# Attention denominators as compact rows spread by DMA broadcasts, the output gate folded into W_o ahead of the merge, and the third modulation set moved into the W_o phase

## The chip, the cores and the metric

The kernel runs on one core of one Trainium2 chip. The metric is device time in microseconds (us), lower is better. Times are quoted as the median of several executions with the lowest and highest beside it. Each experiment was timed beside the kernel before on the same chip in the same rounds. A program on one core can also fall into slower executions; a run is labelled slow when it is more than 1.5% above the fastest run of the same kernel, and the ratios use only the runs that are not.

## The reference

One transformer block: linear attention with 32 heads, then a gated feed-forward network (FFN). Six rows computed from a condition vector `c` scale, shift and gate both halves (the *modulation*).

```python
mod = (silu(c) @ w_mod).reshape(1, 6, 1, 1024)     # sa, ca, ga, sb, cb, gb
h = layernorm(x) * (1 + ca) + sa                   # x: 2048 rows of 1024
q, k, v = split_heads(h @ wqkv)                    # 32 heads of 32 columns
pq, pk = phi(q), phi(k)                            # phi(t) = t+1 or exp(t), positive
kv  = einsum('bhsd,bhse->bhde', pk, v)             # one 32x32 matrix per head
z   = einsum('bhsd->bhd', pk)
num = einsum('bhqd,bhde->bhqe', pq, kv)
den = einsum('bhqd,bhd->bhq', pq, z)[..., None] + 1e-6   # one number per head and row
x = x + ga * ((num / den) @ wo)
h = layernorm(x) * (1 + cb) + sb
x = x + gb * ((gelu(h @ w_gate) * (h @ w_up)) @ w_down)  # F = 3584
```

## The kernel before

**A plan, then in-order engines.** The kernel first *records* every operation and then sorts the list with its own model of the chip (one DMA pipe, fixed latencies). It then issues each engine's operations in that fixed order. On the chip each engine takes its own list strictly in order: an operation that isn't ready holds up everything behind it on the same engine. A change to any operation makes the planner sort anew, so it can move operations in phases that the change doesn't touch. In the experiments, "order frozen" means that the sorted list of another kernel was written into the source as a list of operation numbers, so that only the named edit differs.

**Phases.** (1) LayerNorm, then K, V and Q for four blocks of 512 rows. (2) The merge: each head's KV matrix is multiplied into W_o once (giving `Wp`), interleaved with the last Q blocks and two modulation sets. (3) The W_o phase: 16 tiles of 128 rows, residual add, second LayerNorm; the normalised rows go to DRAM (`xhs`) and come back transposed in two DMA transposes of 1 MB. (4) For each half of the rows (0 and 1), a gate/up phase and a down phase. Both use a Strassen-like scheme, so the kernel needs sums of quarters of the weights. Those of `W_down` (`ts`) are built in DRAM by 28 copy and accumulate DMAs of 256 KB, called the *moves* here.

The denominators before: one block-diagonal matrix `Dbd` per group of four heads, so that a 128x512 matmul yields the denominator already repeated over the 32 rows of its head; then 1/den as exp(-ln(den)) on ACT, over all 128x1024 numbers.

```python
def den_pair(b, g, banks):
    psd = banks.pair()
    for i in range(2):
        te.matmul(psd[:, i, :], lhsT=Dbd[:, g + i, :], rhs=pqT[b][:, g + i, :], start=True, stop=True)
    ac.activation(out=psd, in_=psd, func=AF.Ln, bias=eps6, scale=1.0)
    rden = rden_ring()
    ac.activation(out=rden, in_=psd, func=AF.Exp, scale=-1.0)
    o = pqT[b][:, g:g + 2, :]
    tt_op(o, o, rden, ALU.mult)                     # DVE; 16 such pairs in all

def wp_step(g):                                     # merge: (KV x W_o) x gate row
    psw = psW.pair()
    for h in range(2):
        te.matmul(psw[:, h, :], lhsT=KVbdT[:, g, :], rhs=Wo_sb[:, g, h * NW:(h + 1) * NW], start=True, stop=True)
    ve.scalar_tensor_tensor(out=Wp[:, g, :], in0=psw.rearrange("p h n -> p (h n)"), scalar=1.0 / GA_SCALE,
                            in1=garow, op0=ALU.mult, op1=ALU.mult)

def wo_tile(tt, banks):
    xt = x2_ring()                                  # ring of 4 row buffers
    sy.dma_start(out=xt, in_=x_in[tt * P:(tt + 1) * P, :])
    psw = banks.pair()
    # ... 16 matmuls of pqT[b] with Wp ...
    tt_op(xt, psw.rearrange("p h n -> p (h n)"), xt, ALU.add)      # residual add, DVE
    gp.dma_start(out=x2_scr[b][tl * P:(tl + 1) * P, :], in_=xt)
    # ... ln2_xhat writes the normalised rows to xhs, and every fourth tile:
    sy.dma_start_transpose(out=hr2[:, :, h * TG:(h + 1) * TG], in_=xh_scr[g][h][:])

def plain(name, A, out, start):                     # down phase: load of a W_down quarter or sum
    wt = quarters(...)
    (sy if last or name[0] != "t" else gp).dma_start(out=wt, in_=wd_full[name])
```

`te`, `ve`, `ac`, `gp` and `sy` record for TensorE, VectorE (DVE), ScalarE (ACT), GpSimd (POOL) and SyncE (SP, which issues most DMAs). In the first down phase, loads of the sums `t...` are issued by GpSimd, all other loads by SP.

## Time and profile before

| | before |
|---|---|
| median (lowest to highest), first three runs | 758.01 us (757.61 to 759.67) |
| profiled execution: span, granted TensorE clock | 754.9 us, 1.00 |
| TensorE busy | 734.4 us, 97% of the span |
| W_o phase / gate/up 0 / down 0 | 60.8 / 170.7 / 80.7 us |

The profile page's first part gives, for each engine, busy us, share of the span and number of instructions (PEld is the weight load, which overlaps PE):

```profile
PE 734.4 (97%) x4144; PEld 391.3 (52%) x4164; DVE 623.4 (83%) x1304; ACT 411.6 (55%) x697; POOL 95.8 (13%) x175
```

The view of waits, for TensorE in the kernel before. Columns: what waited, for what, us in total, how often, longest.

```profile
PE psum L648 <- DVE mem L635: 5.5, 1, 5.5
PE psum L685 <- DMA mem<-in_c_dram: 2.2, 1, 2.2
PE psum L964 <- ACT mem L967: 1.9, 2, 1.0
PE psum L952 <- DVE mem L536: 0.7, 1, 0.7
```

The first two lines are the unavoidable start; L964 is the denominators' matmul waiting for ACT (the Exp of L967). TensorE has hardly anything else to wait for. The view by windows, one row per phase (merge and end of Q, W_o, gate/up 0, down 0, gate/up 1). The header names the columns; a number in brackets counts instructions, PEclk is the granted clock and the DMA share is the mean busy share of the 16 DMA engines:

```profile
core 0: us, PE busy (x) PEld busy (x) DVE busy (x) ACT busy (x) POOL busy (x), PEclk, DMA share, GB/s
152.50:192.90 40.40, 37.19 (x241) 17.20 (x244) 35.02 (x59) 31.29 (x36) 15.08 (x16) 1.00 0.89 214
192.90:253.70 60.80, 59.99 (x277) 27.18 (x279) 50.28 (x83) 38.37 (x55) 11.98 (x22) 1.00 0.83 244
253.70:424.40 170.70, 169.26 (x862) 84.06 (x861) 149.26 (x341) 116.99 (x220) 21.70 (x39) 1.00 0.62 204
424.40:505.10 80.70, 80.59 (x519) 50.76 (x520) 64.57 (x117) 19.63 (x30) 6.00 (x9) 1.00 0.86 257
505.10:669.80 164.70, 164.59 (x947) 92.46 (x946) 145.23 (x335) 105.97 (x221) 1.43 (x2) 1.00 0.35 107
```

In the W_o phase TensorE is busy 59.99 of 60.80 us. The timeline of this phase shows how the rows get back (columns: start us, duration us, engine, line, operation, out<-in; SPq is SP issuing a DMA):

```profile
219.25 5.32 SPq L1116 DMA_TRANSPOSE mem<-xhs  x1
225.24 0.42 SPq L1248 DMA_DIRECT2D mem<-in_B_w_gate_dram  x1
229.05 0.80 ACT L1158 ACTIVATE mem<-mem 128x512 f16<-128x512 f16 x1
```

### The profile page before, as it was taken

What the parts mean: (1) busy time and instruction counts of PE and PEld (TensorE: products, weight loads), DVE (VectorE), ACT (ScalarE), POOL (GpSimd) and SP (SyncE); (2) the same over time, 40 slices, a digit from 0 to 9 for tenths busy, and PEclk for the clock granted to TensorE, in tenths of its full rate; (3) what the DMA queues carried; (4) which work ended last, traced back from release to release, by engine and by line L of the source; (5) the groups of instructions that cost most, each with busy time, mean ns of one, the idle gap of its engine ahead of it and who ended that gap; (6) DMA issues with size and microseconds to landing.
All of it is one profiled execution on the core that took longest, in us unless ns stands there. A gap on an engine that the chain in (4) does not pass through costs nothing.

```text
span 754.9 us, 11379 instructions
## 1 busy us (share of the span) xinstructions
PE 734.4 (97%) x4144; PEld 391.3 (52%) x4164; DVE 623.4 (83%) x1304; ACT 411.6 (55%) x697; POOL 95.8 (13%) x175
## 2 busy tenths in 40 slices
PE   5999999998999999999999999999999999999997
PEld 2454544453444444444545486645555555548664
DVE  7898986579897788988998689678888899998763
ACT  3675675668866578766755243016666667621000
POOL 2331332007121003101100001010000000000000
PEclk9999999999999999999999999999999999999999
DMA  9848166789389647687652999752322313399822
GB/s 314 305 120 252 43 151 155 277 309 167 86 231 315 232 154 246 220 272 281 207 185 60 292 276 313 254 181 84 112 78 90 112 56 112 103 274 294 280 95 80
DMA packets 140760, 144.78 MB, mean 192 GB/s; under 512 B 33441, under 2 KB 120865, under 8 KB 139937
## 3 DMA queue, kind: packets, MB, share of 16 engines
q1 hardware_dynamic: 124016, 106.31, 46.8%
q0 software_dynamic: 14336, 35.66, 14.9%
q10 hardware_dynamic: 2352, 2.10, 0.8%
q8 instruction: 32, 0.52, 0.3%
q14 instruction: 24, 0.19, 0.1%
HBM read 111.81 MB, written 32.24 MB: 191 GB/s over the span
## 4 chain that ended last, share of the span: by engine, by line
PE 80%; DVE 8%; ACT 6%; DMA 4%; issue 1%; SPq 1%; DVEq 0%; ACTq 0%
PE psum L1286 28%; PE psum L1489 13%; PE psum L1533 9%; PE psum L1297 7%; DVE mem L536 7%; PE psum L838 6%; PE psum L1178 6%; PE psum L908 4%; PE psum L937 4%; DMA mem<-in_A_wqkv_dram 2%; DMA mem<-in_B_w_up_dram 1%; DMA mem<-in_w_mod_dram 1%; PE psum L952 1%; ACT psum L965 1%; ACT mem L967 1%
## 5 line engine op out<-in xcount | busy, mean ns | idle before, releaser
L536 DVE TENSOR_TENSOR mem<-mem 128x512 f16<-128x512 f16 (+11 forms) x633 | 292.5, 506 | 12.1 <-ACT mem L967 2.5
L1286 PE MATMUL psum<-mem 128*128 128x512 f16 x1248 | 299.3, 379 | 1.3 <-ACT psum L1340 0.5
L536 DVE TENSOR_TENSOR mem<-psum,mem 128x512 f16<-128x512 f32 (+4 forms) x260 | 192.3, 748 | 67.5 <-ACT mem L783 22.6
L783 ACT ACTIVATE mem<-psum 128x256 f32<-128x256 f32 (+2 forms) x228 | 123.2, 555 | 121.1 <-PE psum L1533 46.4
L1286 PEld LDWEIGHTS <-mem 128*128 128x128 f16 (+1 forms) x1248 | 122.0, 98 | 113.4 <-issue 4.0
L1489 PE MATMUL psum<-mem 128*128 128x512 f16 (+2 forms) x458 | 99.0, 372 | 0.7 <-DVE mem L536 0.5
L1297 PE MATMUL psum<-mem 128*128 128x256 f16 x560 | 89.5, 272 | 0.3
L1297 PEld LDWEIGHTS <-mem 128*128 128x128 f16 (+1 forms) x560 | 54.7, 98 | 45.7 <-issue 3.9
L1489 PEld LDWEIGHTS <-mem 128*128 128x128 f16 x462 | 45.1, 98 | 49.9 <-issue 0.7
L1533 PE MATMUL psum<-mem 128*128 128x256 f16 (+1 forms) x588 | 66.2, 273 | 0.0
L1340 ACT ACTIVATE psum<-psum 128x512 f32<-128x512 f32 x56 | 33.0, 589 | 59.0 <-PE psum L1286 31.5
L1533 PEld LDWEIGHTS <-mem 128*128 128x128 f16 x588 | 57.5, 98 | 9.2
L838 PE MATMUL psum<-mem 128*128 128x512 f16 (+1 forms) x272 | 61.6, 379 | 0.4
L1178 PE MATMUL psum<-mem 128*128 128x512 f16 x256 | 57.4, 379 | 0.8 <-DVE mem L536 0.7
L908 PE MATMUL psum<-mem 128*128 128x512 f16 x224 | 51.1, 379 | 0.1
L536 DVE TENSOR_TENSOR psum<-psum,mem 128x256 f32<-128x256 f32 x80 | 34.2, 427 | 12.3 <-ACT mem L783 12.2
L1357 ACT ACTIVATE mem<-psum 128x512 f16<-128x512 f32 x56 | 33.2, 598 | 18.8 <-PE psum L1286 18.3
L838 PEld LDWEIGHTS <-mem 128*128 128x128 f16 x280 | 27.1, 98 | 31.2
L1178 PEld LDWEIGHTS <-mem 128*128 128x128 bf16 x256 | 25.0, 98 | 31.0 <-issue 0.9
L1367 ACT ACTIVATE mem<-mem 128x512 f16<-128x512 f16 x56 | 34.9, 633 | 2.0 <-DVE mem L536 1.8
L908 PEld LDWEIGHTS <-mem 128*128 128x128 f16 (+1 forms) x224 | 21.5, 98 | 26.8 <-issue 2.1
L614 DVE BATCH_NORM_STATS2 mem<-mem 128x6 f32<-128x512 bf16 x48 | 31.0, 678 | 1.6 <-DMA mem<-in_A_x_dram 1.6
(126 smaller groups left out, 558.5 us busy)
## 6 DMA issues: line engine op xcount, KB each, us to landing
mem<-in_B_w_gate_dram SPq DMA_DIRECT2D x14, 1024.0 KB, 6.1
mem<-in_B_w_up_dram SPq DMA_DIRECT2D x14, 1024.0 KB, 5.8
mem<-in_w_mod_dram SPq DMA_DIRECT2D x24, 512.0 KB, 7.0
mem<-us SPq DMA_DIRECT2D x24, 448.0 KB, 8.0
mem<-in_A_x_dram SPq DMA_DIRECT2D x32, 256.0 KB, 4.0
ts<-in_B_w_down_dram POOLq DMA_DIRECT2D x28, 256.0 KB, 6.7
us<-mem POOLq DMA_DIRECT2D x7, 768.0 KB, 7.2
mem<-in_B_w_down_dram SPq DMA_DIRECT2D x12, 448.0 KB, 6.8
```

The costliest lines, as they stand in the source:

```text
L536: ve.tensor_tensor(out=out, in0=a, in1=b, op=op)
L783: ac.activation(out=t, in_=ps, func=AF.Copy)
L838: te.matmul(ps, lhsT=A[:, k, i * P:(i + 1) * P], rhs=B[:, k, :], start=(start and k == 0), stop=(k == KH - 1), skip_group_check=True)
L908: te.matmul(o, lhsT=W[:, k, (j0 + i) * P:(j0 + i + 1) * P], rhs=h_form(a, k), start=(start and k == 0), stop=(k == KH - 1), skip_group_che ...
L1178: te.matmul(psw[:, half, :], lhsT=pqT[b][:, g, tl * P:(tl + 1) * P], rhs=Wp[:, g, half * NW:(half + 1) * NW], start=(g == 0), stop=(g == K ...
L1286: te.matmul(ps, lhsT=a[:, k, e, :], rhs=b[:, k, :], start=(start and k == 0), stop=(k == KH - 1), skip_group_check=True)
L1297: te.matmul(ps, lhsT=self.x[a][:, k, :], rhs=self.y[y][:, k, :], start=(start and k == 0), stop=(k == KH // 2 - 1), skip_group_check=True)
L1340: ac.activation(out=z, in_=x, func=AF.Copy)
L1357: ac.activation(out=o, in_=ps, func=AF.Gelu_apprx_tanh)
L1367: ac.activation(out=o, in_=o, func=AF.Gelu_apprx_tanh)
L1489: te.matmul(psm[:, q, c], lhsT=A[:, i, q * P:(q + 1) * P], rhs=wt[:, i, c], start=(start and i == 0), stop=(i == NPR - 1), skip_group_chec ...
L1533: te.matmul(ps[:, q, :], lhsT=a[:, k, q * P:(q + 1) * P], rhs=y[:, k, :], start=(start and q == 0 and k == 0), stop=(k == NPR // 2 - 1), s ...
```

## The change

Its intent: take denominator work off TensorE (most of the sum's output rows are copies), most of the Ln/Exp off ACT, and the gate's multiply of PSUM off DVE. In detail:

- **Denominators.** 32-column matmuls put the denominators of two blocks compactly into one PSUM bank; one Ln and one Exp of 128x512 serve two blocks; the result goes to DRAM in 4 DMAs of 16 KB and comes back repeated over 32 rows, per block in 4 DMAs of 256 KB.
- **Gate.** W_o is multiplied by the gate row (16 bits, on DVE) before the merge, so the merge's PSUM is evacuated by a plain ACT copy.
- **Third modulation set.** Its load and matmuls go from the merge into the W_o phase.
- **Also in it:** the FFN's up products become an ACT copy and a 16-bit DVE multiply instead of a DVE multiply from PSUM (56 times); the 28 moves, 16 in the K/V/Q phase and 12 in the merge before, are now 14 in the K/V/Q phase and 14 in gate/up 0; the ring of row buffers grows from 4 to 8 and its loads may be issued earlier; the planner learns that the four broadcasts write one tile together. Small parts: the order of the moves, two more PSUM banks for the merge (4 to 7, not 4 and 5), the second modulation set one merge stage later, one more `c1` buffer.

```diff
-    def den_pair(b, g, banks):  (shown above, 16 calls)
+    def den_sums(pr, ps):
+        for gi in range(KH):
+            for b in range(2):
+                for half in range(2):
+                    o, g = DH * (2 * b + half), KH * half + gi
+                    te.matmul(ps[o:o + DH, :], lhsT=zc[:, g, :], rhs=pqT[2 * pr + b][:, g, :],
+                              start=(gi == 0), stop=(gi == KH - 1))
+        ac.activation(out=ps, in_=ps, func=AF.Ln, bias=eps6, scale=1.0)
+        ac.activation(out=rdc, in_=ps, func=AF.Exp, scale=-1.0)
+        # ... 4 writes of rdc to den_scr[pr]
+    def den_mul(b):
+        rden = rden_ring()
+        plan.together(True)
+        for j in range(P // DH):
+            src = den_scr[b // 2][b % 2, j].rearrange("h x -> (h x)")
+            sy.dma_start(out=rden[DH * j:DH * j + DH].rearrange("p g t -> p (g t)"),
+                         in_=src[None, :].to_broadcast((DH, KD * TG)))
+        plan.together(False)
+        for g in range(0, KD, 2):
+            o = pqT[b][:, g:g + 2, :]
+            tt_op(o, o, rden[:, g:g + 2, :], ALU.mult)
 ...
     def wp_step(g):
-            te.matmul(psw[:, h, :], lhsT=KVbdT[:, g, :], rhs=Wo_sb[:, g, h * NW:(h + 1) * NW], ...)
-        ve.scalar_tensor_tensor(out=Wp[:, g, :], in0=psw..., scalar=1.0 / GA_SCALE, in1=garow, ...)
+            te.matmul(psw[:, h, :], lhsT=KVbdT[:, g, :], rhs=Wog[:, g, h * NW:(h + 1) * NW], ...)
+        ac.activation(out=Wp[:, g, :], in_=psw..., func=AF.Copy, scale=1.0 / GA_SCALE)
 ...
     merge_phase, by stage i:
-            i == 3: load of modulation set 2;  i == 11: its matmuls;  i == 12: its columns
-            i in (6, 8, 10, 12, 13): den_pair
+            i == 5: den_sums(0, psN());  i in (8, 11): den_mul;  i == 8: load of modulation set 2
     wo_phase, by tile tt:
-            den_pair at every tile until done
+            tt == 2: matmuls of set 2;  tt == 3: den_sums(1, psX());  tt in (4, 7): den_mul
 ...
-        put(3, 1, F(wd_moves, hr1[3][:, 0, 0:1], 16))      # K/V/Q phase; 12 more in the merge
+            wd_moves(hr1[b][:, 0, 0:1], NPR)               # 14 in the K/V/Q phase
+                wd_moves(w["s1"][:, 0, 0, 0:1], 2)         # 2 per even unit of gate/up 0
 ...
-                    tt_op(o, ps, o, ALU.mult)
+                    tt_op(o, fcopy(c1_ring, ps), o, ALU.mult)
```

## The prediction

> **What bounds the kernel now.** TensorE. The page's first part shows it busy for 734 of 755 us at a granted clock of 1.00; the chain that ended last is 80% TensorE. Of its 20 us idle, about 8.8 lie in the first 25 us and 3.6 in the tail; in the table of 25 us stretches only 175 to 200 stands out between (2.9 us idle; ACT 21.4 and DVE 21.8 of 25 us busy), then 225 to 250 and 275 to 325 (0.5 to 0.7 each). The waits view names the denominators' Exp on ACT (1.9 us of TensorE waits). So time can come only from TensorE work removed or from these small gaps; the large ACT and DVE savings are mostly off the critical path.
>
> **Costs, from the trace.**
> - Denominators. Before: 32 matmuls of 128x512, spaced 0.216 us in an unbroken run: 6.9 us. After: 32 matmuls with 32 output columns; those of the modulation sets run 16 in 0.98 us, so 2.0 us. This fits the Trainium skill, "TensorEngine Tiling (Array Packing)", where narrow tiles run in parallel and a mode switch drains the array; I allow 0.2 us for each of two more switches. About -4.6 us, all critical.
> - ACT: 16 x (Ln 1.09 + Exp 1.02) = 34 us removed; added 2 x (0.6 + 0.6) and, in the merge, 8 copies of 1.02.
> - DVE in the merge: 8 x 1.22 (gate times PSUM) becomes 8 x 0.68 (gate times W_o, 16-bit); the diagonals (8 x 0.24) narrow. About -5 us. The 16 denominator multiplies stay.
> - The third modulation set's matmuls (2 us) only move.
> - DMA: four broadcasts of 1 MB, about 6 us each at the trace's 1 MB landing times, after a write of 2 to 4 us, issued several 2 us stages or 3.9 us W_o tiles before use: at most a short new wait. Of the 28 W_down moves (256 KB), 14 go to the first gate/up phase (DMA share 0.6 to 0.85, loads early): neutral.
> - FFN up products: 56 PSUM multiplies (about 0.7 us of DVE) become an ACT copy (0.6) and a 16-bit multiply (about 0.35): DVE -17 us, ACT +33, but TensorE loses only 1 to 2 us in the first gate/up phase and nearly nothing in the second.
>
> **Sum.** -4.6 from denominators, -2.5 of the 4 us or so lost in the merge, -0.6 in the W_o phase, -0.8 at the start of the FFN: about -8.5 us. Predicted 749.5 us, range 744.5 to 755. Chances: faster by over 2% 0.04, within 2% 0.94, slower 0.02.
>
> **What would show each step.** TensorE's matmul count unchanged, its gap-free time 5 us lower; denominator matmuls about 60 ns apart; ACT partly idle, not 85% busy, in the merge; no TensorE wait for the denominators' Exp; W_o phase starting some 4 us and ending 7 to 8 us earlier; second group's gate/up and down of unchanged length; DVE about 25 us less busy, ACT about level.
>
> **What would make it wrong.** (1) A new wait on the chain gate row, W_o x gate, merge, which starts just after the second half of the modulation set: the merge then gains nothing (about 752). (2) The broadcasts land late, behind the 4 MB of the third modulation set or in order behind other issues of the SP queue, so that the first W_o tile or the modulation matmuls wait several us (755 or more). (3) The new ACT copies hold up the FFN's banks or GELUs. (4) The list order, computed anew, shifts other phases by a us or two.

## The result and the profile after

| | before | after |
|---|---|---|
| median (lowest to highest), 4 runs | 757.81 us (757.08 to 759.67) | 783.78 us (781.66 to 790.27) |
| ratio of fast runs | | 1.035 (1.029 to 1.042) |
| span and clock of the profiled run | 754.9, 1.000 | 779.9, 0.985 |

Ratios are the mean time of one kernel's fast runs over that of the other's of the same rounds, so they are not quite the ratio of the medians quoted. The kernel is 3.5% slower where it was predicted 1.1% faster, and its runs scatter more: 1.1% from lowest to highest against 0.3%.

The first part of the page and the TensorE waits, after:

```profile
PE 737.8 (95%) x4164; PEld 390.8 (50%) x4164; DVE 603.2 (77%) x1304; ACT 417.2 (54%) x733; POOL 101.0 (13%) x179
...
PE psum L1214 <- DVE mem L550: 12.5, 3, 11.1
PE psum L1577 <- ACT mem L799: 5.7, 1, 5.7
PE psum L662 <- DVE mem L649: 5.6, 1, 5.6
PE psum L924 <- DVE mem L550: 2.6, 1, 2.6
PE psum L1329 <- DVE mem L550: 2.6, 1, 2.6
```

The work changed as intended: DVE is 20 us less busy and ACT about level. But TensorE has four new waits: one of 11.1 us in a W_o tile (L1214), one of 5.7 us in down 0 (L1577), and two of 2.6 us (L924 is the merge's Q, L1329 gate/up 0). The same windows by phase, after; the last one is a short stretch around the long wait:

```profile
core 0: us, PE busy (x) PEld busy (x) DVE busy (x) ACT busy (x) POOL busy (x), PEclk, DMA share, GB/s
156.80:190.80 34.00, 31.37 (x192) 13.87 (x192) 24.83 (x49) 25.77 (x32) 0.31 (x1) 0.98 0.62 198
190.80:266.10 75.30, 62.84 (x311) 27.11 (x310) 48.97 (x81) 19.12 (x37) 12.69 (x23) 0.89 0.93 248
266.10:442.00 175.90, 169.34 (x862) 84.10 (x861) 146.36 (x351) 131.40 (x249) 41.33 (x59) 1.00 0.71 215
442.00:529.90 87.90, 82.25 (x521) 51.48 (x520) 67.41 (x125) 19.49 (x30) 6.11 (x9) 0.98 0.87 232
529.90:694.60 164.70, 164.32 (x946) 92.42 (x945) 134.02 (x327) 120.75 (x249) 1.45 (x2) 1.00 0.35 106
244.20:257.90 13.70, 5.05 (x12) 1.72 (x12) 3.72 (x5) 5.75 (x8) 1.08 (x2) 0.50 1.00 243
```

By the phase table below (these windows are rounded) the 25.0 us of span divide as follows: up to the start of the W_o phase -2.1, W_o +14.6, gate/up 0 +5.2, down 0 +7.1, the rest +0.2. The DMA share in the W_o phase rose from 0.83 to 0.93 and PEclk fell to 0.89. In the last row, 13.7 us around the wait, the clock is 0.50.

That is the clock gate. The Trainium skill, "TensorE: Matmul & The Clock Gate", section "What's actually happening", says that an idle window of 3413 ns brings TensorE to half its clock and that a busy window brings it back. This trace agrees on the length of a window. After the start of the kernel, the half-clock stretches last 3.4 us (189.6 to 193.0, and 476.3 to 479.7) and 13.65 us (244.2 to 257.9, four windows); each belongs to one of the waits in the table, and the kernel before has none until its end. It does not show that the window before must be idle throughout. Cut into windows of 3.413 us in step with the start of the half-clock stretch, TensorE was still busy for 1.15 of 3.41 us in the window before the merge's stretch (from 186.23) and for 0.96 before the long one (from 240.84); before that of down 0 it was idle (0.00, from 472.95). The wait of L1329 in gate/up 0, also of 2.56 us, was followed by no half clock; in the corresponding window (367.14 to 370.55) TensorE was busy for 1.54 us. Most of the long stretch is the wait itself, but from 252.85 to 257.9 TensorE works at half clock, which by these numbers costs about 2.5 us more. A wait of a few us can therefore cost more than itself.

### Where the W_o wait comes from

The timeline of the W_o phase, after. A bracket at the end of a line gives the idle time before it and what ended it:

```profile
212.55 3.70 SPq L998 DMA_DIRECT2D mem<-den  x8
219.49 0.38 SPq L1291 DMA_DIRECT2D mem<-in_B_w_gate_dram  x1
225.78 10.96 SPq L1150 DMA_TRANSPOSE mem<-xhs  x1
248.28 5.75 ACT L1192 ACTIVATE mem<-mem 128x512 f16<-128x512 f16 x8 [17.97 <-DMA mem<-xhs]
249.83 1.03 DVE L550 TENSOR_TENSOR mem<-mem 128x512 f16<-128x512 f16 x2 [11.61 <-ACT mem L1192]
251.58 2.35 DVE L550 TENSOR_TENSOR mem<-psum,mem 128x1024 bf16<-128x1024 f32 x2
252.85 9.34 PE L1214 MATMUL psum<-mem 128*128 128x512 f16 x31 [11.05 <-DVE mem L550]
```

Read it downwards. Eight broadcasts (2 MB, blocks 2 and 3) are issued at 212.55, and the planner has now put the gate weights *ahead* of the transpose. The transpose is issued at 225.78, takes SP 10.96 us to issue (5.32 before), and the transposed rows reach ACT 22.5 us after the issue (9.8 before). DVE, in its fixed order, comes to sums that need ACT's result and waits 11.61 us; behind them in its list stand residual adds (L550 from PSUM) that are long ready; TensorE waits 11.05 us for the PSUM banks that those adds would free. The wait named at the end is DVE, but DVE had nothing to do: the origin is a DMA.

The trace's DMA packet records show what the transpose waited for. The broadcasts no longer moved when it was issued: by 225.1 all their packets of 8,192 bytes had started. The gate weights' 1,024 packets of 1,024 bytes ran from 226.7 to 231.1, and the transpose's 4,096 packets of 256 bytes began at 230.9, 5.1 us after its issue (2.2 us in the kernel before). They then took 16.7 us instead of 4.9, mixed with 448 packets of 4,096 bytes, seven row stores of 256 KB issued by GpSimd (44 such packets in the kernel before). So the broadcasts cost time by pushing other transfers, the gate weights and row stores among them, into the transpose's way.

In the merge the same happens in small: DVE waits 6.19 us for a broadcast (the line of 184.74), and TensorE 2.57 us for DVE, followed by 3.4 us at half clock.

```profile
184.74 3.10 DVE L550 TENSOR_TENSOR mem<-mem 128x1024 bf16<-128x1024 bf16 x5 [6.19 <-DMA mem<-den]
188.49 2.48 PE L924 MATMUL psum<-mem 128*128 128x512 f16 x8 [2.57 <-DVE mem L550]
```

### Where the down 0 wait comes from

In down 0 the second half's rows are transposed again, from `xhs`, and the sum `t1` of W_down (1.8 MB) is loaded by GpSimd. First before, then after:

```profile
443.31 0.55 POOL L1485 DMA_DIRECT2D mem<-ts  x1 [51.70 <-PE psum L1533]
444.02 10.70 SPq L1116 DMA_TRANSPOSE mem<-xhs  x1
```

```profile
457.54 7.68 SPq L1150 DMA_TRANSPOSE mem<-xhs  x1
460.91 0.60 POOL L1529 DMA_DIRECT2D mem<-ts  x1 [56.86 <-PE psum L1577]
474.91 1.52 ACT L1192 ACTIVATE mem<-mem 128x512 f16<-128x512 f16 x2 [8.09 <-DMA mem<-xhs]
476.95 3.05 PE L1577 MATMUL psum<-mem 128*128 128x256 f16 x14 [5.65 <-ACT mem L799]
```

Before, `t1` is issued 0.7 us ahead of the second transpose; after, 3.4 us behind it, into the middle of it. The DMA packet records of the trace tell what follows. Before, the 128 packets of 14,336 bytes of `t1` run from 446.0 to 451.8 and that transpose's 256-byte packets after them; only 4 of its 4,096 took over 0.5 us. After, the 256-byte packets run from 461.0 to 471.1, overlap with `t1` from 466.0 on, and 124 of 4,096 took over 0.5 us. `t1` landed after 16.0 us instead of 9.4. ACT waits in order for the transposed rows, and an ACT copy that TensorE needs (L799, at 476.33) stands behind.

A second thing changed here. In the kernel before, the rows of that transpose landed late too, at 458.2, 14.2 us after the issue, and cost TensorE nothing: two of ACT's copies (L783, at 452.68 and 455.28) stood ahead of the rows' readers in its list. So the overlap needs such a list order to become a TensorE wait; no run tests that order alone.

### The profile page after: what moved, and what is told of

Its sections match the earlier page's. It is cut to its first block, busy times and chain, and to the rows that moved or that the text cites. A ratio compares the mean times of both kernels' runs of the same rounds, so it can differ in the third digit from the quotient of the medians.

```text
span 779.9 us, 11464 instructions
## 1 busy us (share of the span) xinstructions
PE 737.8 (95%) x4164; PEld 390.8 (50%) x4164; DVE 603.2 (77%) x1304; ACT 417.2 (54%) x733; POOL 101.0 (13%) x179
## 3 DMA queue, kind: packets, MB, share of 16 engines
q0 software_dynamic: 14336, 35.66, 15.4%
## 4 chain that ended last, share of the span: by engine, by line
PE 61%; DVE 12%; DMA 12%; issue 7%; ACT 5%; POOL 1%; SPq 1%; POOLq 0%; DVEq 0%; ACTq 0%
PE psum L1329 22%; PE psum L1533 12%; DVE mem L550 10%; PE psum L1577 6%; PE psum L1340 6%; PE psum L854 4%; PE psum L953 4%; DMA mem<-in_w_mod_dram 3%; DMA mem<-in_B_w_up_dram 3%; PE psum L924 3%; DMA mem<-xhs 2%; PE psum L677 2%; DMA mem<-den 1%; DMA mem<-ts 1%; ACT mem L799 1%
## 5 line engine op out<-in xcount | busy, mean ns | idle before, releaser
L550 DVE TENSOR_TENSOR mem<-mem 128x512 f16<-128x512 f16 (+10 forms) x697 | 318.5, 503 | 52.9 <-ACT mem L799 13.0
L1329 PE MATMUL psum<-mem 128*128 128x512 f16 x1248 | 299.8, 379 | 4.5 <-DVE mem L550 2.6
L799 ACT ACTIVATE mem<-psum 128x512 f16<-128x512 f32 (+3 forms) x284 | 154.1, 562 | 114.7 <-PE psum L1577 46.1
L550 DVE TENSOR_TENSOR mem<-psum,mem 128x512 f16<-128x512 f32 (+4 forms) x204 | 154.3, 764 | 60.5 <-ACT mem L799 22.7
L1329 PEld LDWEIGHTS <-mem 128*128 128x128 f16 (+1 forms) x1248 | 122.0, 98 | 116.8 <-issue 7.9
L1577 PE MATMUL psum<-mem 128*128 128x256 f16 (+1 forms) x588 | 67.7, 276 | 5.7 <-ACT mem L799 5.7
L1214 PE MATMUL psum<-mem 128*128 128x512 f16 x256 | 60.0, 396 | 12.5 <-DVE mem L550 12.5
L1577 PEld LDWEIGHTS <-mem 128*128 128x128 f16 x588 | 58.2, 99 | 15.6 <-issue 5.8
L924 PE MATMUL psum<-mem 128*128 128x512 f16 x224 | 51.8, 382 | 3.3 <-DVE mem L550 2.6
L550 DVE TENSOR_TENSOR psum<-psum,mem 128x256 f32<-128x256 f32 x80 | 34.3, 428 | 19.1 <-ACT mem L799 18.8
L1214 PEld LDWEIGHTS <-mem 128*128 128x128 bf16 x256 | 25.7, 101 | 46.3 <-issue 19.2
L924 PEld LDWEIGHTS <-mem 128*128 128x128 f16 (+1 forms) x224 | 21.6, 98 | 31.1 <-issue 6.6
L1410 ACT ACTIVATE mem<-mem 128x512 f16<-128x512 f16 x56 | 34.2, 625 | 4.2 <-DVE mem L550 3.7
L1192 ACT ACTIVATE mem<-mem 128x512 f16<-128x512 f16 x28 | 20.6, 802 | 26.1 <-DMA mem<-xhs 26.1
```

The source lines that it names most:

```text
L550: ve.tensor_tensor(out=out, in0=a, in1=b, op=op)
L799: ac.activation(out=t, in_=ps, func=AF.Copy)
L924: te.matmul(o, lhsT=W[:, k, (j0 + i) * P:(j0 + i + 1) * P], rhs=h_form(a, k), start=(start and k == 0), stop=(k == KH - 1), skip_group_che ...
L1214: te.matmul(psw[:, half, :], lhsT=pqT[b][:, g, tl * P:(tl + 1) * P], rhs=Wp[:, g, half * NW:(half + 1) * NW], start=(g == 0), stop=(g == K ...
L1329: te.matmul(ps, lhsT=a[:, k, e, :], rhs=b[:, k, :], start=(start and k == 0), stop=(k == KH - 1), skip_group_check=True)
L1410: ac.activation(out=o, in_=o, func=AF.Gelu_apprx_tanh)
```

## The experiments

The theories that were put to the test are these. **The broadcast theory**: the bytes and the time of the den broadcasts crowd the DMA engines just ahead of the first transpose. **The order theory**, its rival: the change is sound, but the newly planned order (gate weights ahead of the transpose, sums ahead of adds in DVE's list, moves in gate/up 0) costs the time whatever the bytes. **The `t1` theory**: down 0 has a cause of its own, the overlap of the `t1` load with a transpose. **The copies theory**: the new ACT copies hold up gate/up 0. Where an expectation names a theory by a letter, the text beside it says what it blames. Eighteen kernels were run. This is the phase table of all profiled runs that were fast (us from the first matmul of one phase to that of the next; "to W_o" is the time up to the W_o phase):

| kernel | to W_o | W_o | gate/up 0 | down 0 | gate/up 1 | down 1 |
|---|---|---|---|---|---|---|
| before | 192.9 | 60.8 | 170.7 | 80.7 | 164.7 | 82.1 |
| after | 190.8 | 75.4 | 175.9 | 87.8 | 164.8 | 82.2 |
| small_den | 187.8 | 58.8 | 176.3 | 105.4 | 164.8 | 82.1 |
| hold_sums | 188.5 | 64.5 | 183.1 | 88.2 | 164.8 | 82.1 |
| t1_on_sp | 191.1 | 73.2 | 175.2 | 80.8 | 164.9 | 82.1 |
| moves_early | 195.0 | 76.2 | 174.7 | 87.3 | 164.8 | 82.1 |
| small_den_t1 | 187.0 | 58.8 | 177.3 | 81.5 | 164.9 | 82.1 |
| small_den_t1_moves | 193.0 | 61.4 | 174.4 | 80.7 | 164.9 | 82.1 |
| small_den_t1_nocopy | 186.6 | 58.8 | 181.4 | 80.8 | 167.0 | 82.1 |
| den_only | 196.0 | 70.1 | 173.2 | 80.7 | 164.7 | 82.2 |
| den_only_small | 191.4 | 68.8 | 173.4 | 80.7 | 164.7 | 82.1 |
| v2a | 190.8 | 68.2 | 178.5 | 81.2 | 164.5 | 82.1 |
| v2b | 189.8 | 62.3 | 178.1 | 80.9 | 166.0 | 82.1 |
| h1 | 190.6 | 59.4 | 174.5 | 80.9 | 166.4 | 82.1 |
| h2 | 190.1 | 64.5 | 175.1 | 80.8 | 165.4 | 82.1 |
| h3 | 190.1 | 59.7 | 182.5 | 80.9 | 166.4 | 82.1 |
| h5 | 190.8 | 58.7 | 172.6 | 80.7 | 164.7 | 82.1 |
| h6 | 189.6 | 59.3 | 171.8 | 80.7 | 164.7 | 82.1 |

### Four single edits to the kernel after, its order otherwise frozen

**small_den**: the broadcasts carry a quarter of their bytes (and the multiply uses those for all groups; wrong, though the output still passed the tolerance).

```diff
-            sy.dma_start(out=rden[DH * j:DH * j + DH]..., in_=src[None, :].to_broadcast((DH, KD * TG)))
+            sy.dma_start(out=rden[DH * j:DH * j + DH, 0:2]..., in_=src[None, 0:2 * TG].to_broadcast((DH, 2 * TG)))
-            tt_op(o, o, rden[:, g:g + 2, :], ALU.mult)
+            tt_op(o, o, rden[:, 0:2, :], ALU.mult)
```

> The changed kernel with every engine's instruction order frozen as it was; each denominator broadcast moves 2 KB a row and not 8 KB (0.25 MB and not 1 MB a block; wrong result on purpose). Theory A (the broadcasts' bytes fill the DMA engines ahead of the first transpose of the normalised rows, which landed 22 us after its issue and not 10, and DVE waits in order for what it feeds): the 11 us TensorE wait in the W_o phase shrinks below 5 us, the 2.7 us one in the merge goes, about 762 to 768 us. Rival B (the new list order is at fault, whatever the bytes): under 3 us gained, about 780 us.

Measured: 772.73 us (769.5 to 780.09), ratio 1.022 (1.016 to 1.028). The W_o phase falls from 75.4 to 58.8 us, shorter than before's 60.8, and the start of it from 190.8 to 187.8: with an unchanged order and unchanged instruction counts, the bytes alone were worth 19.5 us (266.1 less 246.6) up to the end of W_o in the profiled runs. The total gained less than the 762 to 768 us expected, because down 0's wait grew. In the profiled run, the slowest of the four, down 0 took 105.4 us:

```profile
452.26 16.92 SPq L1574 DMA_DIRECT2D mem<-in_B_w_down_dram  x2
473.38 1.52 ACT L1199 ACTIVATE mem<-mem 128x512 f16<-128x512 f16 x2 [25.73 <-DMA mem<-xhs]
475.43 3.02 PE L1584 MATMUL psum<-mem 128*128 128x256 f16 x14 [23.29 <-ACT mem L806]
```

The load of `t1` landed 31.3 us after its issue, the transpose's 256-byte packets were spread from 442 to 472, and 15 of the 128 packets of 14,336 bytes took 4.7 to 9.0 us (none over 1.1 in the kernel before). So down 0 is a separate cause, and one whose size differs from run to run. That is a reason for the scatter of the kernel after.

**hold_sums**: two sums in DVE's list (inner sums of the FFN's right operand) moved behind the residual add of W_o tile 13; nothing else.

```diff
 FROZEN = [order of the kernel after], with
-    ..., sum, sum, add of tile 13, ...
+    ..., add of tile 13, sum, sum, ...
```

> The changed kernel, order frozen, with just two DVE instructions (the first two sums of the inner split of h2) moved behind the add of W_o tile 13. Rival B (DVE's order: these two wait for the late transpose while adds that are ready stand behind them): TensorE no longer waits 11 us at W_o tile 13, it waits later, at the start of the FFN, for h2; about 6 to 10 us gained, 772 to 777 us. Theory A alone (all is the late transpose): the wait only moves, under 4 us gained.

Measured: 780.97 us (773.07 to 800.96), two of four runs slow; ratio of the fast ones 1.023 (1.020 to 1.026). The transpose is as late as before the edit (issued 224.40, its reader on ACT at 246.87, again 22.5 us), but TensorE's W_o waits fall to 2.7 us in total and the phase to 64.5 us. So the in-order list of DVE is what turned a late transpose into a TensorE wait. But gate/up 0 then took 183.1 us instead of 175.9: part of the gain was given back where the late rows are used next.

**gate_late**: the first gate weight load moved behind the first transpose in SP's list. **gate_den_late**: the four broadcasts of the last block as well.

```diff
 FROZEN = [order of the kernel after], SP's list:
-    den x8, gate weights, x row, transpose 0
+    den x8, x row, transpose 0, gate weights               (gate_late)
+    den x4, x row, transpose 0, gate weights, den x4       (gate_den_late)
```

> The changed kernel, order frozen, with one instruction moved: the 1 MB load of the first gate weights is issued after the first transpose of normalised rows, as in the kernel before, and not ahead of it. Theory A (DMA traffic ahead of the transpose): the transpose lands about 3 to 5 us earlier and about as much is gained, 775 to 779 us. Rival B: nothing gained.

> As the run with the gate weights moved, and the four broadcasts of the last block's denominators (1 MB), which are needed only at W_o tile 12, are moved behind that transpose too. Theory A: the transpose lands 7 to 10 us earlier, the W_o stall falls to under 3 us and its half-clock stretch goes, 768 to 773 us. Rival B: as changed kernel, about 780 us, or later if the last block's broadcasts now come too late.

Measured: gate_late 782.54 us (773.44 to 806.37), two runs slow, ratio of the fast ones 1.032 (1.028 to 1.035): no clear change against the kernel after. gate_den_late 774.66 us (771.37 to 794.24), one run slow, ratio 1.022 (1.019 to 1.024). Neither median reached what the broadcast theory expected (775 to 779, and 768 to 773). Both profiles are of runs labelled slow, and the label goes by time alone. What they show is a lead and no proof: most of their excess stands in down 0 (about 115 and 106 us), where TensorE waits 33.2 and 23.0 us for ACT as under the `t1` theory, while W_o takes 72.9 and 69.8 us. In gate_late the transposed rows reached ACT 12.4 us after the issue although all eight broadcasts went before it, and DVE then waited 8.64 us for the gate weights. So the gate weights' place may have a large part in the late transpose. Down 0's varying wait is in the fast runs too, so their totals only hint that moving the broadcasts as well helped. The broadcast theory rests on small_den. The order theory keeps a share: hold_sums shows that the same late data hurts more or less depending on the lists.

### Testing the down 0 cause, the moves and the copies

**t1_on_sp**: `t1` is issued by SP, so that it comes after the transpose in one list; order frozen.

```diff
-            (sy if last or name[0] != "t" else gp).dma_start(out=wt, in_=wd_full[name])
+            (sy if last or name[0] != "t" or name == "t1" else gp).dma_start(out=wt, in_=wd_full[name])
```

> The changed kernel, order frozen; one DMA changes its queue: the 1.8 MB load of W_down's t1 form in the first down phase goes to the SP queue, right behind the second DMA transpose of the late rows, and not to the GpSimd queue, where its 14 KB packets run in the middle of that transpose[...]. Theory C (this collision delays the transpose, ACT waits in order for it, TensorE for ACT): the 5.7 to 33 us TensorE wait in the first down phase falls under 3 us, the scatter of the runs from some 10 us to under 4, the median to 772 to 777 us. Rival: the transpose is late from the traffic as a whole, and then both stay.

Measured: 772.13 us (770.61 to 774.84), ratio 1.019 (1.017 to 1.022). Down 0 falls to 80.8 us, the wait is gone, and the runs scatter by 4 us instead of 9. The packet records show why: the 14,336-byte packets start at 464.5, the moment the last 256-byte packet starts. This settles the `t1` theory: 7.0 of the 25 us in the profiled runs, about 11.7 between the medians (783.78 less 772.13, from different rounds).

The Trainium skill, "DMA: Bandwidth & Descriptors", section "Issuing engines are not separate DMA queues", says that DMAs of all issuing engines run on the same 16 DMA engines and interleave. This agrees, and shows the price: 1.8 MB issued by GpSimd held up a transpose issued by SP.

**moves_early**: the 14 moves of gate/up 0 placed into the merge (after steps 1 to 5 of it), order otherwise frozen.

```diff
 FROZEN = [order of the kernel after], with
-    14 moves, 2 per even unit of gate/up 0
+    14 moves behind wp_step 1..5
```

> The changed kernel, order frozen, but the 14 moves of W_down that it issues in the first gate/up phase are issued in the merge, where the kernel before had them. If they cause the 9 us of TensorE gaps of the first gate/up phase (4 in the kernel before), these fall to about 5, and 3 to 5 us are gained if nothing is lost in the merge. If the ACT copies of the up products cause them, nothing is gained.

Measured: 789.93 us (784.9 to 794.7), ratio 1.042 (1.037 to 1.048), the slowest of all. Gate/up 0 gains 1.2 us, the time to W_o loses 4.2. TensorE's merge wait grows from 2.6 to 6.3 us. Beside the broadcasts and in this order the merge has no room for these bytes; the kernel before had 12 of the moves there. Whether taking them out of the merge helps without the broadcasts is not shown.

**small_den_t1**: small_den and t1_on_sp together. **small_den_t1_moves**: and moves_early. **small_den_t1_nocopy**: small_den_t1, with the FFN up products multiplied from PSUM as before (its output is wrong as small_den's, here with a relative error of 0.022, over the tolerance).

```diff
 small_den_t1 = small_den + t1_on_sp
 small_den_t1_moves = small_den_t1 + moves_early
 small_den_t1_nocopy = small_den_t1 +
-                    tt_op(o, fcopy(c1_ring, ps), o, ALU.mult)
+                    tt_op(o, ps, o, ALU.mult)
```

> Both remedies: a quarter of the broadcasts' bytes (wrong on purpose) and the t1 load on the SP queue; order frozen. Theories A and C together: W_o and down phases without a wait over 3 us, 751 to 756 us. If the losses were due to the list order whatever the DMA does, it stays over 762 us.

> As the run with both remedies, and the 14 W_down moves issued in the merge too. If the three causes are all there is, the compute side of the change is left alone: 747 to 751 us, what was predicted for the whole change. Otherwise over 753 us.

> As the run with a quarter of the broadcasts' bytes and the t1 load on the SP queue, order frozen, but the 56 ACT copies of the up products are left out: DVE multiplies from PSUM as in the kernel before. If these copies (DVE gets ahead and then waits in order for weights that have not landed) make the first gate/up phase 177 us long and not 171 as before, it comes back to 171 to 173 and the run to 750 to 753 us. If they are neutral or help, 756 to 760 us.

Measured: small_den_t1 756.54 us (754.82 to 757.89), ratio 0.998 (0.996 to 1.000). Its phases:

```profile
core 0: us, PE busy (x) PEld busy (x) DVE busy (x) ACT busy (x) POOL busy (x), PEclk, DMA share, GB/s
156.30:187.00 30.70, 30.65 (x192) 13.81 (x191) 25.01 (x49) 25.19 (x31) 0.31 (x1) 1.00 0.56 197
187.00:245.80 58.80, 58.80 (x311) 26.27 (x310) 49.29 (x81) 19.64 (x38) 12.83 (x23) 1.00 0.87 254
245.80:423.10 177.30, 170.82 (x862) 84.48 (x861) 146.80 (x351) 131.46 (x249) 41.28 (x59) 0.99 0.72 220
423.10:504.60 81.50, 80.85 (x521) 50.77 (x520) 67.48 (x125) 19.39 (x30) 5.55 (x8) 1.00 0.86 249
```

This is the key run. With the broadcast bytes and the `t1` overlap out of the way, the end of the W_o phase comes at 245.8 instead of 253.7, 7.9 us earlier; the prediction's terms for the work up to there (4.6 + 2.5 + 0.6) sum to 7.7. TensorE is busy in every us of the phase (58.80 of 58.80). So the sum of removed and added *work* was right (its parts weren't measured apart, and the broadcasts here are too small on purpose), and the kernel after loses it to *data arriving late*. What stays is gate/up 0, 177.3 us against 170.7.

small_den_t1_moves: 759.96 us (757.48 to 763.25), ratio 1.003 (0.999 to 1.007). Gate/up 0 gains 2.9 us, the time to W_o loses 6.0 and W_o 2.6. Even with small broadcasts the merge doesn't have room for the moves.

small_den_t1_nocopy: 759.04 us (756.52 to 761.42), ratio 1.001 (0.996 to 1.005). Without the copies gate/up 0 takes 181.4 us, 4.1 more, in an order planned for copies. The copies theory falls: the copies aren't what makes gate/up 0 longer.

### The denominators alone

**den_only**: the kernel before with only the new denominators, replanned. **den_only_small**: its order frozen and a quarter of the bytes (wrong, within the tolerance).

```diff
 den_only = kernel before, with den_sums/den_mul of the change (merge stage 5, W_o tile 3;
            multiplies at merge stages 8, 11 and W_o tiles 4, 7), no other part of it
 den_only_small = den_only, order frozen, with the edit of small_den
```

> The kernel before with one part of the change alone: the denominators in compact rows and their broadcasts; its list order is computed anew. If the broadcasts are the chief cause, it is slower than the kernel before although TensorE has 5 us less to do: 762 to 775 us, with a wait in the W_o phase. If another part is, 752 to 757 us.

> The kernel before with the denominators' part alone, its own list order frozen, and a quarter of the bytes in each broadcast (wrong on purpose). If the bytes cost the time: W_o loses under 2 us, 752 to 758 us, 15 us or more under the run with the full broadcasts. If the order does: over 765 us.

Measured: den_only 772.94 us (771.55 to 773.68), ratio 1.019 (1.015 to 1.022). So the denominators alone make the kernel before slower; no other part of the change is needed. Its time to W_o is 196.0 and W_o 70.1 us; gate/up 0 takes 173.2 and down 0 80.7. den_only_small: 768.4 us (765.87 to 769.4), ratio 1.013 (1.011 to 1.016), and this was a miss for the broadcast theory: fewer bytes gave 4.6 us at the start of W_o but only 1.3 in the W_o phase, which stayed at 68.8. TensorE's waits in the W_o tiles (L1208, and L1215 in the second) hardly moved. First den_only, then den_only_small; L1005 is the merge:

```profile
PE psum L1208 <- DVE mem L547: 9.2, 3, 3.7
PE psum L1005 <- DVE mem L1006: 5.4, 3, 4.7
```

```profile
PE psum L1215 <- DVE mem L554: 8.7, 3, 3.7
```

In this kernel, then, something other than bytes makes the W_o tiles wait. It keeps the ring of 4 row buffers where the change has 8, and it was suspected that SP, which issues in order, holds up row loads behind broadcasts that wait for their slot. The traces don't bear this out: SP's broadcasts wait 0.8 us for DVE in both runs, and its row loads wait 17 us for stores of rows, less than the 28.7 us in the kernel before, which has the same ring. In the trace of den_only_small the waits come out of DVE's list: at 210.74 TensorE waits 3.29 us for multiplies by the denominators that stand behind some 6 us of other DVE work without a gap, and at 255.51 3.73 us for an add that stands behind sums of the late transposed rows. That is a reading of one trace; no run tests it, and it stays open. It also means that "bytes" is shown as the cause for the kernel after (small_den) and not for any kernel with broadcasts.

### Repairs: a version that keeps the gain

**v2a**: the kernel after with the third modulation set back in the merge, PSUM banks 4 and 5 for the merge, the second denominators earlier (W_o tile 1; multiplies at tiles 2 and 4), their two buffers used in the order 0, 0, 1, 0, their loads allowed earlier, the first gate weights held behind the first transpose, `t1` on SP; replanned. **v2b**: v2a without the FFN copies.

```diff
+        plan.ahead = 24000                       # den loads may be issued earlier
-            if tt == 3:  den_sums(1, psX())      ... if tt in (4, 7): den_mul
+            if tt == 1:  den_sums(1, psX())      ... if tt in (2, 4): den_mul
-    psX, psW, psN = Banks(4, 7), Banks(4, 7), Banks(6, 7)
+    psX, psW, psN = Banks(4, 7), Banks(4, 5), Banks(6, 7)
+        if g == 0:
+            plan.hold(h2_loads[0, 0])            # gate weights behind the transpose
 (t1 on SP; set 2 back in the merge; v2b: tt_op(o, ps, o, ALU.mult))
```

> A repair, list order computed anew, result right: third modulation set back in the merge (its 4 MB load ahead of the first broadcasts), second pair of denominators summed at W_o tile 1 and not 3, its slots swapped so that one broadcast need not wait, first gate weights held behind the first transpose, t1 load on the SP queue. If DMA timing is what cost the time, W_o loses under 5 us: 750 to 760 us. If not, over 765 us.

> The same repair with DVE multiplying the up products from PSUM, as in the kernel before: 2 to 5 us less than the repair with the copies if these lengthen the first gate/up phase, 747 to 757 us; the same or more if they help.

Measured: v2a 765.87 us (764.11 to 770.08), ratio 1.009 (1.005 to 1.012); v2b 766.03 us (764.0 to 766.51), ratio 1.009 (1.006 to 1.013). Both beat the kernel after by about 18 us (in different rounds) and missed what was hoped for: v2a lies in the range that its expectation kept for "not DMA timing". Down 0 is cured (81.2 and 80.9). W_o is 68.2 and 62.3 us, and gate/up 0, at 178.5 and 178.1, loses most. Blocks 2 and 3 still fetch 2 MB ahead of the transpose, which may be why W_o is long; no run shows it, and 4.1 us of v2a's W_o waits come before the early sums. The copies again make no difference to the total.

So the broadcast was kept only where it does no harm. **h1**: blocks 0 and 1 (in the merge) by broadcast, blocks 2 and 3 by the old `den_pair`; the third modulation set in the merge; gate weights held; `t1` on SP; no FFN copies; all 28 moves before the merge. **h2**: h1 with the copies. **h3**: h1 with 14 moves left in gate/up 0.

```diff
-    den_todo = list(range(NG))
+    den_todo = [0, 1]                                                   # by broadcast
+    pair_todo = [(b, g) for b in range(2, NG) for g in range(0, KD, 2)] # by den_pair, W_o tiles
+        put(3, 6, F(wd_moves, hr1[3][:, 0, 0:1], NPR))                  # second 14 moves
-                wd_moves(w["s1"][:, 0, 0, 0:1], 2)
 h2:  + tt_op(o, fcopy(c1_ring, ps), o, ALU.mult)
 h3:  - put(3, 6, ...);  + wd_moves(w["s1"][:, 0, 0, 0:1], 2)
```

> A second repair, result right: only blocks 0 and 1 get their denominators by broadcast, in the merge; blocks 2 and 3 by TensorE and ACT in the W_o phase, as in the kernel before (3.5 us of TensorE, less 1 us saved); third modulation set in the merge; first gate weights behind the first transpose; t1 load on the SP queue; all 28 W_down moves ahead of the merge; no ACT copies of the up products. If the broadcasts ahead of the transposes are the cause, the W_o phase is 61 to 64 us long and the first gate/up phase 171 to 174: 750 to 757 us. If the moves now collide in the merge: 757 to 765.

> As h1, with the ACT copies of the up products. If they help the first gate/up phase, 1 to 4 us less than h1; if they lengthen it, 2 to 5 us more.

> As h1, but 14 of the W_down moves stay in the first gate/up phase, as in the changed kernel. If they lengthen that phase, it is 3 to 6 us longer than in h1; if not, the same within 1.5 us.

Measured: h1 759.51 us (756.55 to 764.28), ratio 1.002 (0.998 to 1.007); h2 761.6 us (761.03 to 762.49), ratio 1.005 (1.003 to 1.006); h3 767.5 us (766.17 to 769.42), ratio 1.013 (1.011 to 1.016). W_o is 59.4 us in h1, with no large wait. In h2 it is 64.5 although its edit touches only FFN operations: the planner's new order again. h3 differs from h1 by 14 moves, and gate/up 0 takes 182.5 instead of 174.5 us. Each of the two was planned anew, so these 8.0 us hold the moves and a new order; in the frozen orders above taking the moves away was worth 1.2 and 2.9 us. So the moves in gate/up 0 are not neutral. In h1 gate/up 0 runs the same FFN operations as the kernel before, and still takes 174.5 us against 170.7. The order of the lists is the chief difference left there.

**h5 and h6** test that: h1's program (with `t1` on GpSimd as before), but from the FFN on the lists follow the order of the kernel *before*, joined at the first FFN matmul (h5) or 220 matmuls later (h6).

```diff
 h5: FROZEN = [order of h1 up to the first FFN matmul] + [order of the kernel before from there]
 h6: the same, joined 220 matmuls later
+            (sy if last or name[0] != "t" else gp).dma_start(...)      # t1 as before
```

> The program of h1 (t1 load back on the GpSimd queue, as before), with each engine's order of the FFN's instructions taken from the kernel before, from the FFN's first matmul on. If the list order is what lengthens the first gate/up phase, it is 170 to 172 us long, both gate/up phases as in the kernel before, and the run 750 to 754 us, under 757.5. If something else does, 173 us or more and 756 to 760.

> As h5, joined 220 matmuls later, so that the passage from W_o to the FFN keeps the order of h1. By list order alone: 750 to 755 us; if the passage is where h1 loses its 4 us, slower than h5 by 1 to 3 us.

Measured, five rounds beside the kernel before (757.63 us): h5 754.16 us (752.41 to 756.33), ratio 0.995 (0.993 to 0.997); h6 752.13 us (749.95 to 752.82), ratio 0.992 (0.990 to 0.994). Gate/up 0 falls to 172.6 and 171.8 us, gate/up 1 from 166.4 to 164.7. h5 just missed its expectation for gate/up 0 (170 to 172) and the total (750 to 754). For the same operations the order was worth 1.9 to 2.7 us in gate/up 0 and 1.7 in gate/up 1; the other edit, `t1` back on GpSimd, acts only in down 0. TensorE's waits in h6:

```profile
PE psum L670 <- DVE mem L657: 5.3, 1, 5.3
...
PE psum L1348 <- DVE mem L558: 1.2, 1, 1.2
```

Apart from the start, nothing over 1.2 us is left in gate/up. h6 is correct and beats both kernels. Against before it is 0.8%, clear of the noise.

## Why the prediction was wrong

The prediction was 749.5 us, the result 783.78. In the profiled runs the error is 33.5 us: 25.0 slower instead of 8.5 faster. It divides as 20.2 us up to the end of W_o (+12.5 instead of -7.7), 6.0 in gate/up 0 (+5.2 instead of -0.8), 7.1 in down 0 and 0.2 in the rest.

**The step that failed** was the DMA term of the costs: "four broadcasts of 1 MB, about 6 us each at the trace's 1 MB landing times ... at most a short new wait". Two things in it were wrong.

- *It asked when the broadcasts would arrive and not what they would delay.* The first parts of each burst landed about as estimated: 5.6 us in the median of the four landings of 16 that the view of the `den` tile has. By the packet records the last parts came later, 7.1 and 7.7 us after their issue in the merge and 9.7 in W_o. In the W_o phase, with DMA 83% busy before, they pushed the gate weights and row stores into the way of the 1 MB transpose, whose rows came 22.5 us after its issue instead of 9.8; three in-order lists (SP, ACT, DVE) carried that to TensorE as a wait of 11.05 us, and the clock gate added about 2.5 us of half-speed work behind it. small_den shows it: the same order with a quarter of the bytes gives a W_o phase of 58.8 us.
- *It spoke of DMA only in the phases that the change edits.* No edit names down 0; only the order of the lists changed there, and it lost 7.1 us to the overlap of `t1` with a transpose. t1_on_sp shows it. Neither the prediction nor its list of risks has this.

**"Of the 28 W_down moves, 14 go to the first gate/up phase ...: neutral"** was wrong too. With the order frozen, taking them out was worth 1.2 and 2.9 us there. The rest of gate/up 0's 6.0 us is not fully accounted for; order has a part, for the FFN of h1, h5 and h6 is the same and takes 174.5, 172.6 and 171.8 us. The last 1.1 us of h6 against before was not traced.

**What was named as a risk.** "(2) The broadcasts land late ..., so that the first W_o tile or the modulation matmuls wait several us (755 or more)" names the right suspect. The place was another (tiles behind the transpose, not the first), the way was another (what they delayed, not their own landing), and the wait, 11.05 us, was larger than "several us". "(4) The list order, computed anew, shifts other phases by a us or two" was right in kind and too small in size: 1.9 to 2.7 us in gate/up 0 by order (h5, h6), and 5.1 us in the W_o phase of h2, planned anew for the copies. "(3) The new ACT copies hold up the FFN's banks": did not happen; without them gate/up 0 is 4.1 us longer in that order, and h2 has about h1's (175.1 and 174.5).

**What was right.**

- The TensorE work. 16 denominator matmuls take 1.05 us (the first set of the W_o phase, below), 2.1 us for all 32 against the 6.9 of before. The Trainium skill, "TensorEngine Tiling (Array Packing)", "Key Properties", says that tiles run in parallel; this trace agrees: four of the narrow matmuls start within 10 ns and the next four 0.21 us later, so a matmul takes 66 ns where a full one takes 216. The two switches cost about 0.19 us a set (the steps into and out of it are 0.309 and 0.312 us), close to what the prediction allowed.
- The sum up to the end of W_o, -7.7 us, against -7.9 measured once the data came in time (small_den_t1).
- "Second group's gate/up and down of unchanged length": 164.7 and 82.1 became 164.8 and 82.2. ACT "about level" (411.6 and 417.2), DVE 20 us less busy (25 predicted).

```profile
204.30 1.05 PE L983 MATMUL psum<-mem 128*32 128x512 bf16 x16
```

**What stays open.** Whether den_only's W_o tiles wait almost as long with a quarter of the bytes because of DVE's list. How much of the first transpose's delay is due to the gate weights' place, and how row stores slow its packets: with a quarter of the bytes in the same order they take 6.9 us, among 129 packets of stores. What happens inside the DMA engines when 256-byte transpose packets meet 14,336-byte ones; that the overlap costs time is shown, the mechanism isn't. Why the same overlap cost 6 us in one run and 23 in another. Whether ACT's list order alone would cure down 0. The gate fold and the larger ring of row buffers were never run alone.

## What to carry to other kernels

Before adding DMA bytes to a phase, read that phase's DMA share and list what else is waiting for the same 16 engines there, transposes above all: ask what the new transfer will delay or push aside, not only when it will land. On in-order engines, follow the delayed result down each list to the first thing that TensorE needs behind it, and count some half-speed work on top of any TensorE wait of a few us. When a planner reorders everything, freeze the old order first: only then does an experiment say what the edit costs and what the order costs.

## What the Trainium skill lacked or had wrong

- "DMA: Bandwidth & Descriptors", "Rules for kernel authors", says "A transpose next to ordinary DMAs needs nothing". The rule is about correct results, and these runs agree. What it lacks is the time: behind 2 MB of broadcasts and a 1 MB load the rows of a 1 MB transpose came 22.5 us after its issue instead of 9.8, its packets taking 16.7 us instead of 4.9; and a 1.8 MB load issued 2.9 us into a transpose landed after 31.3 us instead of 9.4, the transposed rows with it. Issued by the same engine after the transpose, the load cost nothing.
- The same page, "Latency and other measured facts", gives 261 GB/s as the effective bandwidth of one DMA transpose with a non-contiguous middle dimension, which would be an estimated 4.0 us for 1 MB. The packets of the first one took 4.9 us in the kernel before, which doesn't contradict it. What the page lacks is a figure for the wait before and among them in a loaded phase: from issue to the first use of the rows it was 9.8 us before and 22.5 after.
- No page has what a zero-stride broadcast read from DRAM costs: the first parts of a burst, 256 KB onto 32 partitions, landed in a median of 5.6 us (3.9 to 6.9, four landings), its last parts 7.1 to 9.7 us after their issue; with 64 KB parts the first ones took 3.6 us (1.9 to 5.0, four landings).
- "TensorE: Matmul & The Clock Gate", Part 1, was right on the window of 3413 ns. What these runs add are numbers for a window that isn't idle throughout. One wait of 2.57 us, with TensorE busy for 1.15 us of the window, was followed by a window at half clock (189.6 to 193.0), another of 2.56 us, with 1.54 us busy, was not; and around one wait of 11.05 us the clock stayed at half for four windows (244.2 to 257.9), the last 5.05 us of them with matmuls running.
